# Linear attention, then a GELU layer: chunk 2's first product by seven half-size products throughout, with half of w_in's block sums formed during chunk 0

## The chip, the cores and the metric

The kernel runs on one core of one Trainium2 chip. A core has TensorE (PE in the profile; its weight loads are PEld), VectorE (DVE), ScalarE (ACT), GpSimd (POOL) and SyncE (SP), which here only issues DMAs. Matmuls write to PSUM, which has eight banks of 128 partitions x 512 fp32; POOL does not read them in this kernel. The metric is the device time of one execution in microseconds; less is better.

## The reference

```python
def _attn_ref(q, k, v):                      # 8 x 8 heads x 576 x 64
    q_s = np.exp(q - np.max(q, axis=-1, keepdims=True))
    q_s = q_s / (np.sum(q_s, axis=-1, keepdims=True) + 1e-09)
    k_s = np.exp(k - np.max(k, axis=2, keepdims=True))
    k_s = k_s / (np.sum(k_s, axis=2, keepdims=True) + 1e-09)
    kv = np.einsum('bhsd,bhse->bhde', k_s, v)
    return np.einsum('bhsd,bhde->bhse', q_s, kv)

x = attn_out.transpose(0, 2, 1, 3).reshape(4608, 512)
h = x @ w_in                                 # 512 x 2048
g = 0.5 * h * (1.0 + erf(h * inv_sqrt2))
return g @ w_out                             # 2048 x 512
```

Inputs and output are float32 in HBM. The kernel multiplies in bf16 and leaves out the subtraction of the maxima, which cancels.

## The kernel before

**Chunks.** The 4608 rows are worked on in nine chunks of 512. Chunk b (0 to 7) is the first 512 rows of batch b; chunk 8 is the 64 rows that each batch has left. A chunk goes through these steps: load q, k, v; exp of q and k on ScalarE (`exp_q`, `exp_k`), cast of v; `norm_q` (VectorE sums exp(q) over a head and takes the reciprocal, L260 and L261; POOL or VectorE multiplies, L262); transposition of q (on TensorE for chunks 0 and 1, by a DMA on SP from chunk 2 on, `xbar_step`, L312); k-v products (`kv_mm`, L225) with a column of ones in v that gives the sums of exp(k); `kv_norm` (reciprocal of that column, L239, and multiply, L240); x transposed (`x_mm`, L332), copied to SBUF by ScalarE (L359) and VectorE (L357) in four blocks of 128 model columns; h with GELU on ScalarE; then the output matmuls, and stores on SP. `manual_schedule` leaves every engine's instructions in the order in which the program writes them.

**h, plain.** Chunks 0 and 1, and half of chunk 2, form h by tiles of 128 of the 2048 columns: four matmuls of 512 columns (the rows of x) each over the four blocks of x (`h_mm`, L366), then one gelu (L372). Chunk 0 does so in `h_phase`, chunk 1 in `h_pairs` with three banks in turn.

**h, by half-size products.** `h_waves` forms h from chunk 2 on by the Winograd form of Strassen's scheme: instead of eight block products seven, each with 256 columns. The h tiles go in four blocks q = 0 to 3 (each: two tiles of the upper and two of the lower half of h). `mm(m, q)` is product m of block q: four matmuls (L486). It needs block sums of w_in (`quad_weights(w)`, four VectorE operations L419; w = 0 serves blocks 0 and 1, w = 1 blocks 2 and 3) and block differences of x (`x_sums`, four VectorE operations t1 to t4). Around the products: `seed` copies product 1 on ScalarE to a second bank (L494), before later products go on adding to the first; `p5_copy` brings product 5 to SBUF (L498); `e_sum` and `r_sum` are VectorE sums (L419) of two or three products; `gelu` finishes the four quarters C, r, B and A (L510). Products 1, 6, 7 and 4 of a block add up in one bank (A), 5, e and 3 use another (B), the seed and 2 a third (C). `roles` names the banks; some serve as C of one block and B of another: C of block 2 is B of block 0.

With `two` true (chunks 3 to 8) both halves of h go through this scheme. With `two` false (chunk 2), blocks 0 and 1 are eight plain tiles, and VectorE forms `quad_weights(0)` meanwhile; blocks 2 and 3 go by products.

**Output.** Chunk 0 multiplies plainly (L607): 16 h tiles x 4 row groups j, into four banks `yps` that the banks' rotation gives: 0, 1, 3, 4. Chunk 0's last h tiles 14 and 15 lie in banks 0 and 1. Among these output matmuls chunk 1's transposition, k-v products and x are placed (its transposes in banks 5 and 2), and chunk 1's first four h tiles lie in banks 0, 1, 3 and 4. From chunk 1 on `y_phase` forms the output by seven half-size products too (L664; `y_last`, L734, for chunk 8); its argument hangs further work behind numbered steps. In chunk 1 step 3 is the k-v step of chunk 2, exp(k) and `norm_q(3)`, whose multiply is POOL's; step 6, at the end, has load(4), x of chunk 2, the transposition of chunk 3's q, and the k-v step of chunk 3. In front of step 5 POOL forms two differences of the output (L419) that the stores wait for.

**Workspace.** The pool `wst` has five slots in rotation for raw weights and later for the sums: w_in parts 0 to 4, w_out parts 0 to 3, w16 (sums of w_out, `mix_wo`), quad_s of w = 1, quad r, quad t, quad_s of w = 0.

Of the kernel before, what the change touches and what calls it, by code (L numbers as in the profile page):

```python
# [8 lines left out]
FP32 = mybir.dt.float32  # L9
BF16 = mybir.dt.bfloat16  # L10
AF = mybir.ActivationFunctionType
ALU = mybir.AluOpType
# [4 lines left out]
def kernel(  # L17
# [212 lines left out]
    def kv_norm(b, half=None):  # L230

        if half is None:
            parts = [(ps, kvc[b][:, 2 * i:2 * i + 2], 2) for i, ps in enumerate(st[b]["kvall"])]
        else:
            parts = [(st[b]["kv"][hp].unsqueeze(1), kvc[b][:, hp:hp + 1], 1)
                     for hp in (2 * half, 2 * half + 1)]
        for src, dst, m in parts:
            rec = small.tile([128, 2], FP32, tag="reck")
            nc.vector.reciprocal(rec[:, 0:m], src[:, :, D])  # L239
            nc.vector.tensor_tensor(  # L240
                out=dst, in0=src[:, :, 0:D],
                in1=rec[:, 0:m].unsqueeze(2).to_broadcast([128, m, D]), op=ALU.mult,
            )
# [7 lines left out]

    def norm_q(b, i=0, n=1, eng=None):

        eng = eng or nc.gpsimd
        eq = st[b]["eq"]
        w = H // n
        hs = slice(i * w, (i + 1) * w)
        qsum = small.tile([128, J, w], FP32, tag="qsum")
        recq = small.tile([128, J, w], FP32, tag="recq")
        nc.vector.reduce_sum(out=qsum, in_=eq[:, :, hs, :], axis=AX.X)  # L260
        nc.vector.reciprocal(recq, qsum)  # L261
        eng.tensor_tensor(  # L262
            out=eq[:, :, hs, :], in0=eq[:, :, hs, :],
            in1=recq.unsqueeze(3).to_broadcast([128, J, w, D]), op=ALU.mult,
        )
# [95 lines left out]
    def h_begin(c):  # L361
        st[c]["g"] = moe_sb.tile([128, NDF, M], BF16, tag="g", name="g", bufs=1)
# [36 lines left out]
    def h_pairs(c, ins, done=()):  # L399


        if not done:
            h_begin(c)
        for p in range(HK):
            for t in (p + HK, p):
                if t in done:
                    continue
                ps = psum_h.tile([128, M], FP32, tag="h", name="ps")
                h_mm(c, ps, t, range(NDM))
                h_gelu(c, ps, t)  # L410
            if p in (1, 3, 5):
                s_ops(c, p - 1, 2)
            elif p > 5:
                s_ops(c, p, 1)
            for f in ins.get(p, []):
                f()
# [36 lines left out]
    def h_waves(c, two, sums):  # L453
# [38 lines left out]
        def seed(q):  # L492
            take("C", q)
            nc.scalar.copy(out=held["C", q], in_=held["A", q])  # L494

        def p5_copy(q, eng):
            held["r", q] = quad["r"][:, q]
            eng(out=held["r", q], in_=held["B", q])  # L498

        def e_sum(q):  # L500
            tt(held["B", q], held["A", q], held["r", q])
# [11 lines left out]
        if two:  # L513
            mm(1, 0, 1)
            seed(0)
            mm(5, 0, 1)
            seed(1)
            p5_copy(0, scopy)
            p5_copy(1, scopy)
            mm(6, 0, 1)  # L520
            x_sums(c, (3,))
            e_sum(0)
            e_sum(1)
            x_sums(c, (4,))
            mm(2, 0, 1)
            gelu("C", 0, 1)
            mm(7, 0, 1)
            r_sum(0)
            r_sum(1)
            mm(3, 0, 1)  # L530
            for q in (2, 3):
                mm(5, q)
                mm(1, q)
            mm(4, 0, 1)
            gelu("r", 0)
            gelu("B", 0, 1)
            gelu("r", 1)
            seed(2)
            seed(3)
            gelu("A", 0, 1)  # L540
            p5_copy(2, vcopy)
            p5_copy(3, vcopy)
            s_parts(c, 0, 4, (3,))
        else:
            turn = Banks(*(roles[n] for n in ("bb", "kv0", "kv1", "x0")))
            x_sums(c, (1, 2, 3, 4))
            for p in range(HK // 2):
                for t in (p + HK, p):
                    ps = turn.tile([128, M], FP32)
                    h_mm(c, ps, t, range(NDM))  # L550
                    h_gelu(c, ps, t)
                if p == 1:
                    s_parts(c, 0, 2, (0, 1))
                    for fn in sums:
                        fn()
            mm(1, 2, 3)
            seed(2)
            seed(3)
            mm(5, 2, 3)
            p5_copy(2, vcopy)  # L560
            p5_copy(3, scopy)
# [3 lines left out]
        if two:  # L565
            s_parts(c, 0, 4, (4,))
# [10 lines left out]
        if two:  # L577
            s_parts(c, 0, 4, (0,))
        else:
            s_parts(c, 2, 2, (0, 1))  # L580
# [346 lines left out]
    def ybank():  # L927
        return psum_y.tile([128, M], FP32, tag="y", name="ps")

    h_phase(0, {  # L930
# [3 lines left out]
        9: [lambda: cast_wo(0, wo[0])],  # L934
# [14 lines left out]
    w16 = wst.tile([128, 2, HK, HN], BF16, tag="w", name="w16")  # L949
    mix_wo(6, 0)  # L950
    mix_wo(6, 1)
# [3 lines left out]
    tps = [pool.tile([128, HP, J, 64], BF16, tag=tag, name="tp")  # L955
           for pool, tag in ((psum_a, "a"), (psum_h, "h"))]
    yps = [psum_h.tile([128, DM], FP32, tag="h", name="ps") for j in range(2)]
    yps += [psum_y.tile([128, DM], FP32, tag="y", name="ps") for j in range(2)]
# [25 lines left out]
    x_tile(1, 0, psum_a, "a")  # L984
    x_tile(1, 1, psum_h, "h")
# [11 lines left out]
    hps = [psum_h.tile([128, M], FP32, tag="h", name="ps") for t in range(2)]  # L997
    hps += [psum_y.tile([128, M], FP32, tag="y", name="ps") for t in range(2)]
# [8 lines left out]
    x_evac(1, 3)  # L1007
    for t in range(2, 4):
        h_mm(1, hps[t], t1s[t], (0, 1))
    for t in range(4):  # L1010
# [8 lines left out]
    sums = quad_weights(1)  # L1019
# [3 lines left out]
    h_pairs(1, h1, done=t1s)  # L1023
# [10 lines left out]
        3: [lambda: kv_step(2), lambda: exp_k(3), lambda: norm_q(3)],  # L1034
        4: [lambda: table(AF.Gelu)],
        6: [lambda: load(4), lambda: x_all(2, (3, 4, 1, 5)), lambda: xbar_step(3), lambda: kv_step(3)],
    })
    quad["r"] = wst.tile([128, 4, 2, HT], FP32, tag="w", name="r")
    quad["t"] = wst.tile([128, 4, 2, HT], BF16, tag="w", name="quad_t")
    sums = quad_weights(0)  # L1040


# [16 lines left out]
    for c in range(2, B + 1):  # L1059
        nb = c + 2  # L1060
        if 2 < c and nb < B:
            load(nb)
        elif nb == B:
            load_qrest()
        h_waves(c, c > 2, sums)
        s_parts(c, 4, 4, (2,))
        yi = {}
        if nb <= B:
            yi[8] = [lambda: exp_q(nb)]
            yi[1] = [lambda: norm_q(nb)]  # L1070
            yi[3] = [lambda: table(AF.Gelu)]
        if nb < B:
            yi[9] = [lambda: exp_k(nb)]
            yi[0] = [lambda: touch_g(c), lambda: cast_v_all(nb)]
        if c < B:
            yi[5] = [lambda: next_x(c, nb)]
            y_phase(c, yi)
        else:
            y_last(c)
# [30 lines left out]
```

## Time and profile before

| what | value |
|---|---|
| time, median of 3 runs (lowest, highest) | 259.36 us (259.2, 259.4) |
| the profiled execution's time | 259.4 us |
| its span, first to last instruction | 257.6 us |
| mean granted clock of TensorE | 0.995 |
| DMA queue q1 | 49.39 MB, 56.9% of 16 engines' span |
| HBM read, written | 36.70 MB, 9.44 MB |
| chunk 0's h matmuls (L366) | 64 in 13.99 us |
| gelu of a plain h tile (L372), mean | 600 ns |
| one half-size matmul (L486) on the row, mean | 273 ns |
| seed (L494), p5 copy on ScalarE (L498), mean | 577 ns, 610 ns |
| e sum, r sum on VectorE (L419), mean | 694 ns, 685 ns |
| block sum of w_in on VectorE (L419), mean | 684 ns |
| POOL multiply of q, 128x2048 (L262, with the half-size ones), mean | 3046 ns |

A row of the profile gives line, engine, operation, tiles and shapes. Matmuls overlap: one of 512 columns shows 379 ns in its row, and 64 of them in a row take 13.99 us; times of TensorE's work are therefore taken from the chain of work that ended last, whose columns are start, duration, and what. In the timeline the columns are start, duration, engine, line, operation, tiles, and count; in square brackets is how long the engine stood idle before, and what released it.

### The profile page before, as it was taken

The numbers are of one execution on the slowest core, as the hardware profiler recorded it, in microseconds if no ns is written. First come the engines' busy times: TensorE is split into PE (matmuls) and PEld (weight loads), VectorE is DVE, ScalarE is ACT, GpSimd is POOL, SyncE is SP. The second block draws the span as 40 slices with busy tenths as digits, with TensorE's granted clock in tenths as the row PEclk, the third lists the DMA queues.
The fourth block names the chain that finished last, engine by engine and source line by source line (L and its number), as shares of the span: only waits on it lengthen the run. The fifth ranks groups of instructions, "written<-read, shape, count | busy, mean of one in ns | idle before, by whom it ended". The sixth has DMA issues, their size and how long they took to land.

```text
span 257.6 us, 6452 instructions
## 1 busy us (share of the span) xinstructions
PE 249.9 (97%) x2646; PEld 193.3 (75%) x2646; DVE 207.2 (80%) x360; ACT 187.8 (73%) x317; POOL 67.6 (26%) x64
## 2 busy tenths in 40 slices
PE   7899999999999999999999999999999999999992
PEld 3444445448856888888888888888888888888881
DVE  1877596998989988898889888988898889398961
ACT  4875986699967996889688968896886687158620
POOL 1530033000790058005800580058001800040000
PEclk9999999999999999999999999999999999999998
DMA  7999999992408964990499039904920440031024
GB/s 234 401 399 427 398 409 398 397 413 118 84 3 272 377 128 90 305 383 3 91 308 368 17 82 307 387 3 86 274 55 0 87 160 3 0 120 46 3 63 101
DMA packets 43165, 50.22 MB, mean 195 GB/s; under 512 B 20224, under 2 KB 30464, under 8 KB 42880
## 3 DMA queue, kind: packets, MB, share of 16 engines
q1 hardware_dynamic: 42736, 49.39, 56.9%
q10 hardware_dynamic: 400, 0.43, 0.7%
q8 instruction: 20, 0.33, 0.5%
q14 instruction: 9, 0.07, 0.1%
HBM read 36.70 MB, written 9.44 MB: 179 GB/s over the span
## 4 chain that ended last, share of the span: by engine, by line
PE 93%; DMA 4%; POOL 1%; ACT 0%; DVE 0%; issue 0%; SPq 0%
PE qa L486 18%; PE ps L366 14%; PE ya L664 10%; PE yd L664 9%; PE qb L486 9%; PE ye L664 5%; PE ps L607 5%; PE yb L664 5%; PE qc L486 4%; PE yx L664 4%; PE ps L332 2%; DMA f<-in_v_dram 2%; PE kv L225 2%; DMA f<-in_q_dram 2%; PE ya L734 1%; PE yd L734 1%
## 5 line engine op out<-in xcount | busy, mean ns | idle before, releaser
L664 PEld LDWEIGHTS <-g 128*128 128x128 bf16 x448 | 43.3, 98 | 5.8 <-issue 0.4
L262 POOL TENSOR_TENSOR e<-e,recq 128x2048 bf16<-128x2048 bf16 (+1 forms) x9 | 27.4, 3046 | 75.1 <-DVE recq L261 50.3
L486 PEld LDWEIGHTS <-quad_s 128*128 128x128 bf16 x416 | 40.7, 98 | 4.9 <-issue 0.2
L664 PEld LDWEIGHTS <-s 128*128 128x128 bf16 x336 | 32.8, 98 | 3.8
L366 PE MATMUL ps<-xT,wi_bf 128*128 128x512 bf16 x160 | 35.5, 379 | 0.1
L486 PEld LDWEIGHTS <-wi_bf 128*128 128x128 bf16 x312 | 30.5, 98 | 3.7
L366 PEld LDWEIGHTS <-wi_bf 128*128 128x128 bf16 x160 | 15.4, 98 | 19.2 <-issue 0.8
L372 ACT ACTIVATE g<-ps 128x512 bf16<-128x512 f32 x40 | 22.5, 600 | 9.1 <-PE ps L366 8.7
L486 PE MATMUL qa<-quad_t,quad_s 128*128 128x256 bf16 x208 | 27.1, 273 | 0.0
L419 POOL TENSOR_TENSOR y_sb<-y_sb 128x512 f32<-128x512 f32 x14 | 19.5, 1394 | 21.8 <-DVE y_sb L419 21.3
L260 DVE TENSOR_REDUCE qsum<-e 128x16 f32<-128x1024 bf16 (+1 forms) x12 | 20.9, 1738 | 4.9 <-ACT e L173 4.8
L494 ACT COPY qc<-qa 128x512 f32<-128x512 f32 x26 | 13.9, 577 | 11.5 <-PE qa L486 11.5
L173 ACT ACTIVATE e<-f 128x512 bf16<-128x512 f32 (+1 forms) x42 | 20.5, 556 | 1.5 <-DMA f<-in_q_dram 1.1
L510 ACT ACTIVATE g<-r 128x512 bf16<-128x512 f32 x26 | 16.2, 630 | 6.6 <-DVE r L419 6.6
L419 DVE TENSOR_TENSOR qb<-qa,r 128x512 f32<-128x512 f32 x26 | 16.9, 694 | 4.6 <-ACT g L510 3.1
L510 ACT ACTIVATE g<-qc 128x512 bf16<-128x512 f32 x26 | 14.1, 594 | 7.2 <-PE qc L486 7.2
L190 POOL CAST v_aug<-f 128x576 bf16<-128x576 f32 x26 | 17.6, 708 | 4.7 <-DMA f<-in_v_dram 4.7
L178 ACT ACTIVATE ek<-f 128x2304 bf16<-128x2304 f32 (+1 forms) x10 | 17.2, 1734 | 0.5 <-DMA f<-in_k_dram 0.5
L419 DVE TENSOR_TENSOR r<-qa,r 128x512 f32<-128x512 f32 x26 | 16.7, 685 | 0.7 <-PE qa L486 0.4
L391 DVE TENSOR_TENSOR s<-g 128x1024 bf16<-128x1024 bf16 x26 | 17.2, 686 | 0.0
L1046 POOL CAST scr<-g 128x1 f32<-128x1 bf16 x4 | 0.7, 187 | 58.6 <-DVE g L394 58.6
L607 PE MATMUL ps<-wo_bf,g 128*128 128x512 bf16 x64 | 14.5, 379 | 0.5 <-ACT g L372 0.5
(96 smaller groups left out, 477.7 us busy)
## 6 DMA issues: line engine op xcount, KB each, us to landing
out_dram<-y_sb SPq DMA_DIRECT2D x16, 512.0 KB, 3.8
f<-in_k_dram SPq DMA_DIRECT2D x6, 1152.0 KB, 9.7
f<-in_v_dram SPq DMA_DIRECT2D x6, 1152.0 KB, 11.7
f<-in_q_dram SPq DMA_DIRECT2D x6, 1024.0 KB, 8.0
w<-in_moe_w_in_dram SPq DMA_DIRECT2D x6, 512.0 KB, 8.7
f<-in_v_dram SPq DMA_DIRECT2D x8, 288.0 KB, 6.2
f<-in_q_dram SPq DMA_DIRECT2D x4, 512.0 KB, 8.9
w<-in_moe_w_out_dram SPq DMA_DIRECT2D x2, 1024.0 KB, 11.8
```

Of the source, the lines that this page charges most:

```text
L173: nc.scalar.activation(out=dst[:, i], in_=src[:, u], func=AF.Exp)
L178: nc.scalar.activation(out=ek[b % 2][:, i:i + n], in_=st[b]["kf"][:, i:i + n].rearrange("p x (n d) -> p x n d", n=NS), func=AF.Exp,)
L190: eng.tensor_copy(out=o, in_=i)
L260: nc.vector.reduce_sum(out=qsum, in_=eq[:, :, hs, :], axis=AX.X)
L262: eng.tensor_tensor(out=eq[:, :, hs, :], in0=eq[:, :, hs, :], in1=recq.unsqueeze(3).to_broadcast([128, J, w, D]), op=ALU.mult,)
L366: nc.tensor.matmul(ps, wi_bf[:, dm, t * 128:(t + 1) * 128], st[c]["xT"][:, dm, :], start=(dm == 0), stop=(dm == NDM - 1),)
L372: nc.scalar.activation(out=st[c]["g"][:, t, :], in_=ps, func=AF.Gelu)
L419: eng.tensor_tensor(out=out, in0=in0, in1=in1, op=op)
L486: nc.tensor.matmul(held[kind, q][:, u], w, mov[m][:, k], start=(m in (1, 5) and u == 0 and k == 0), stop=(k == 1), skip_group_check=True,)
L510: nc.scalar.activation(out=g[:, t:t + 2, half], in_=held[kind, q], func=AF.Gelu)
L607: nc.tensor.matmul(ps, st[c]["g"][:, t, j * 128:(j + 1) * 128], wo_bf[:, t, :], start=(t == 0), stop=(t == NDF - 1),)
L664: nc.tensor.matmul(ps[:, j * HN:(j + 1) * HN], act[m][:, k, j * 128:(j + 1) * 128], wgt[m][:, k, :], start=(first and k == 0 and j == 0), ...
```

## The change

- `kv_norm` for half a chunk's heads takes both reciprocals first and then both multiplies.
- `norm_q` is split in `q_sums` (VectorE) and `q_scale` (the multiply). For chunk 3, `q_sums` stays in chunk 1's `y_phase`; `q_scale` and `xbar_step` go to `q_late`, which is called inside chunk 2's `h_waves`; a small POOL copy there waits for the first p5 copy.
- `h_waves` has no plain tiles any more. In chunk 2 (`mid` given) products 1 of all four blocks come first, then 2, 5, and 6 of blocks 0 and 1, then product 5 of blocks 2 and 3; t1 and t2 are formed around `kv_step(3)` at the end of chunk 1's `y_phase`, t3 and t4 ahead of the e sums. Its p5 copies are all ScalarE's.
- `quad_weights(0)` is formed in chunk 0: two operations behind h tile 9, ahead of the cast of w_out's part 0, and two behind the first `mix_wo`.
- Chunk 0's output lies in banks 3, 4, 2, 0; chunk 1's transposes in 5 and 1; its first four h tiles in 3, 4, 1, 7; its other h tiles take banks 2, 0, 5, 6 in turn.

```diff
     def kv_norm(b, half=None):
...
+        if half is not None:
+            hps = (2 * half, 2 * half + 1)
             rec = small.tile([128, 2], FP32, tag="reck")
+            for i, hp in enumerate(hps):
+                nc.vector.reciprocal(rec[:, i:i + 1], st[b]["kv"][hp][:, D:D + 1])
+            for i, hp in enumerate(hps):
+                nc.vector.tensor_tensor(
+                    out=kvc[b][:, hp, :], in0=st[b]["kv"][hp][:, 0:D],
+                    in1=rec[:, i:i + 1].to_broadcast([128, D]), op=ALU.mult,
+                )
+            return
...
-    def h_waves(c, two, sums):
+    def h_waves(c, mid):
...
-        if two:
-            mm(1, 0, 1)
-            seed(0)
+        mm(1, 0, 1)
+        seed(0)
+        if mid:
+            seed(1)
+            mm(1, 2, 3)
+            mm(2, 0, 1)
+            gelu("C", 0, 1)
+            mm(5, 0, 1)
+        else:
             mm(5, 0, 1)
             seed(1)
-            p5_copy(0, scopy)
-            p5_copy(1, scopy)
-            mm(6, 0, 1)
-            x_sums(c, (3,))
-            e_sum(0)
-            e_sum(1)
+        p5_copy(0, scopy)
+        p5_copy(1, scopy)
+        mm(6, 0, 1)
+        x_sums(c, (3, 4) if mid else (3,))
+        e_sum(0)
+        e_sum(1)
+        if not mid:
             x_sums(c, (4,))
+        if mid:
+            mid()
+            mm(5, 2, 3)
+            p5_copy(2, scopy)
+            p5_copy(3, scopy)
+        else:
             mm(2, 0, 1)
             gelu("C", 0, 1)
...
+        mm(7, 0, 1)
+        r_sum(0)
+        r_sum(1)
+        mm(3, 0, 1)
+        if not mid:
             for q in (2, 3):
                 mm(5, q)
                 mm(1, q)
...
+        mm(4, 0, 1)
+        gelu("r", 0)
+        gelu("B", 0, 1)
+        gelu("r", 1)
+        seed(2)
+        seed(3)
+        gelu("A", 0, 1)
+        if not mid:
             p5_copy(2, vcopy)
             p5_copy(3, vcopy)
-            s_parts(c, 0, 4, (3,))
-        else:
-            turn = Banks(*(roles[n] for n in ("bb", "kv0", "kv1", "x0")))
-            x_sums(c, (1, 2, 3, 4))
-            for p in range(HK // 2):
-                for t in (p + HK, p):
-                    ps = turn.tile([128, M], FP32)
-                    h_mm(c, ps, t, range(NDM))
-                    h_gelu(c, ps, t)
-                if p == 1:
-                    s_parts(c, 0, 2, (0, 1))
-                    for fn in sums:
-                        fn()
-            mm(1, 2, 3)
...
+        s_parts(c, 0, 4, (3,))
         mm(6, 2, 3)
...
+    sums0 = quad_weights(0)
     h_phase(0, {
...
-        9: [lambda: cast_wo(0, wo[0])],
+        9: sums0[0:2] + [lambda: cast_wo(0, wo[0])],
...
     mix_wo(6, 0)
+    for fn in sums0[2:]:
+        fn()
     mix_wo(6, 1)
...
-    tps = [pool.tile([128, HP, J, 64], BF16, tag=tag, name="tp")
-           for pool, tag in ((psum_a, "a"), (psum_h, "h"))]
-    yps = [psum_h.tile([128, DM], FP32, tag="h", name="ps") for j in range(2)]
-    yps += [psum_y.tile([128, DM], FP32, tag="y", name="ps") for j in range(2)]
+    tps = [psum.tile([128, HP, J, 64], BF16, tag=f"k{i}", name="tp") for i in (5, 1)]
+    yps = [bank(i) for i in (3, 4, 2, 0)]
...
-    hps = [psum_h.tile([128, M], FP32, tag="h", name="ps") for t in range(2)]
-    hps += [psum_y.tile([128, M], FP32, tag="y", name="ps") for t in range(2)]
+    hps = [bank(i) for i in (3, 4)]
...
+    hps += [bank(i) for i in (1, 7)]
...
-    h_pairs(1, h1, done=t1s)
+    h_pairs(1, h1, done=t1s, turn=Banks(2, 0, 5, 6))
...
-        3: [lambda: kv_step(2), lambda: exp_k(3), lambda: norm_q(3)],
+        3: [lambda: kv_step(2), lambda: exp_k(3), lambda: q_sums(3)],
         4: [lambda: table(AF.Gelu)],
-        6: [lambda: load(4), lambda: x_all(2, (3, 4, 1, 5)), lambda: xbar_step(3), lambda: kv_step(3)],
+        6: [lambda: load(4), lambda: x_all(2, (3, 4, 1, 5)),
+            lambda: kv_step(3, lambda: x_sums(2, (1,))), lambda: x_sums(2, (2,))],
     })
...
+    def q_late():
+        nc.gpsimd.tensor_copy(out=scr[:, 2:3], in_=quad["r"][:, 0, 0, 0:1])
+        q_scale(3, nc.gpsimd)
+        xbar_step(3)
...
-        h_waves(c, c > 2, sums)
+        h_waves(c, q_late if c == 2 else None)
```

## Prediction

> **What bounds the kernel.** I read the engine totals first, then the chain of work that ended last in order of time, then the timeline of the stretches that the change touches.
>
> ```profile
> PE 249.9 (97%) x2646; PEld 193.3 (75%) x2646; DVE 207.2 (80%) x360; ACT 187.8 (73%) x317; POOL 67.6 (26%) x64
> ```
> ```profile
> 12.89 1.36 PE ps L332 x8
> ...
> 14.26 13.99 PE ps L366 x64
> 28.25 0.02 issue
> 28.27 0.60 ACT g L372
> 28.88 0.04 issue
> 28.92 12.03 PE ps L607 x55
> ...
> 73.34 1.12 PE ps L366 x4
> 74.46 0.01 issue
> 74.48 6.22 PE ps L366 x28
> 80.69 0.87 PE qa L486 x8
> ```
>
> From 12.42 us to 252.67 us the chain is TensorE almost without a break. So a step counts only if it takes matmul time out, or closes or opens a pause of TensorE. The chain shows the few pauses: at L332 eight matmuls take 1.36 where later groups of eight take 0.56; at 28.25 it goes over to ScalarE for a gelu; at 73.34 four matmuls take 1.12 where 64 in 13.99 give 0.218 each, so 0.87. An eight of 256-column products is 0.873 ("a unit" below: 14 of them in 12.23).
>
> **Chunk 0's output in other banks.** Before, the second output matmul needs bank 1, which the gelu of the last h tile (28.27 to 28.87) still reads. TensorE is done with h at 28.25, runs one output matmul (0.22, to 28.47) and goes on at 28.92: a pause of 0.45. Then 55 matmuls take 12.03 against 55 x 0.2177 = 11.97, so 0.06 at most is refill. After, the order is banks 3, 4, 2, 0; the last of them to come free is bank 0, read by the gelu of tile 14, which starts at 27.41 and lasts 0.60: long over when the fourth matmul is due at 28.9. Gain 0.45 to 0.51; I take **-0.48**. What is late next is the data behind it: the last two casts of w_out end at 40.92 and the last v casts at 42.60, both led by DMA; their users (the last tile's matmuls near 42.8, k-v matmuls at 43.90) move to about 42.2 and 43.3. Margin 0.7.
>
> **kv_norm, reciprocals first.** Only its half form (chunks 0 and 1) changes, and only chunk 0 has TensorE waiting for it.
>
> ```profile
> 12.37 0.17 DVE L239 RECIPROCAL rec<-kv 128x1 f32<-128x1 f32 x1 [0.61 <-PE kv L225]
> 12.57 0.22 DVE L240 TENSOR_TENSOR kvc<-kv,rec 128x64 bf16<-128x64 f32 x1
> 12.71 0.16 DVE L239 RECIPROCAL rec<-kv 128x1 f32<-128x1 f32 x1
> 12.90 0.22 DVE L240 TENSOR_TENSOR kvc<-kv,rec 128x64 bf16<-128x64 f32 x1
> ```
>
> A multiply starts 0.20 after its own reciprocal, but an independent operation 0.14 after the one in front. With both reciprocals first the second multiply would start at 12.37 + 3 x 0.14 = 12.79 instead of 12.90: 0.11 sooner. ScalarE's first x copy (13.63) and the first h matmul (14.26) follow it by as much. The trace has no two neighbouring reciprocals: at 0.20 apart nothing is gained; at 0.08 (what 0.16 leaves after the 0.08 that the row shows neighbours to overlap) the last multiply ends 0.26 sooner. Range 0 to 0.26; I take the row: **-0.11**. The Trainium skill (VectorE: DVE Perf Modes, The DRAIN you can't avoid) says that chained operations pay the flush whether or not a semaphore stands between them, so that only their count matters; by it this step would be worth 0. The starts 0.14 and 0.20 apart in these rows speak against it for such short operations, and taking it would raise the sum by 0.11.
>
> **w_in's sums for columns of chunk 2's first half.** Four operations of 0.685 (quad_s<-wi_bf) leave chunk 2 on VectorE for chunk 0. Two stand ahead of the cast of w_out's first quarter, which idled 1.43 for its DMA until 25.87: they need 1.37. Two stand after the first mix, where VectorE then idled 2.87 (for ScalarE's cast, until 30.69). Both covered: **0**. Without cover, the first pair would push that cast from 27.10 towards 28.5, 0.4 beyond the first output matmul. The workspace slots rotate otherwise, but each new owner's predecessor has been cast by then.
>
> **q's scaling and transposition of chunk 3, moved.** One POOL multiply (3.62 at 71.15) moves behind the first p5 copy of chunk 2 (about 77.2) and ends near 81; the transposing DMA on SP stands behind it, at about 81.2, now after load(4) as it was before (it was issued at 81.54 and done by 92). Its reader, chunk 3's x matmul, is at 97.29. On POOL the two output differences no longer wait behind the multiply, so chunk 1's stores and load(4), both queued on SP behind them, go some 3 us sooner. Nothing of this is on TensorE's path: **0**; it would cost only if the transposition came 5 us later than now. Chunk 1's four h banks instead of three: its last 60 h matmuls run 13.06, 0.218 each, so there was no wait to remove: **0**.
>
> **Chunk 2.** Before, eight plain tiles take from 73.34 to 80.69 = 7.35 (32 matmuls are 6.99; the rest is the wait for kv_norm's bank at 74.47 and the refill). After, seven products of two blocks take 7 units = 6.11. Gain **-1.24**. The first product needs only x blocks 0 and 1 (VectorE's first copy ends at 73.40): no wait worth counting. VectorE's differences, e and r sums are each ready 0.2 or more ahead of their product. But look at product 6 of blocks 2 and 3. It accumulates onto banks that ScalarE must first copy (the seed, L494), and the seeds stand behind four gelus. Chunk 3 of before has that same ScalarE order:
>
> ```profile
> 103.72 1.04 PE L486 MATMUL qa<-quad_t,quad_s 128*128 128x256 bf16 x8
> 104.36 1.29 DVE L419 TENSOR_TENSOR r<-qa,r 128x512 f32<-128x512 f32 x2
> 105.08 0.63 ACT L510 ACTIVATE g<-r 128x512 bf16<-128x512 f32 x1 [0.43 <-DVE r L419]
> 105.61 1.07 ACT L510 ACTIVATE g<-qb 128x512 bf16<-128x512 f32 x2
> 106.57 0.63 ACT L510 ACTIVATE g<-r 128x512 bf16<-128x512 f32 x1
> 107.09 1.08 ACT L494 COPY qc<-qa 128x512 f32<-128x512 f32 x2
> ```
>
> Product 7's first half ends at 103.88 (the chain's start of that piece) + 0.44 = 104.32; the first seed ends at 107.09 + 0.60 = 107.69: 3.37 of r sum, gelu r, two gelus B, gelu r, seed, without a hole on ScalarE. In chunk 3 TensorE has between them the other half of product 7 (0.44), product 3 (0.87), products 5 and 1 of blocks 2 and 3 (1.75) and product 4 (0.87): 3.93, so it never waits. In the new chunk 2, products 1 and 5 of blocks 2 and 3 have been drawn ahead and 0.44 + 0.87 + 0.87 = 2.18 is left. TensorE stands for 3.37 - 2.18 = 1.19, plus 0.05 from gelu end to matmul (28.87 to 28.92) and 0.06 of refill: **+1.30**. Behind the seeds on ScalarE stand only gelus A, which nobody awaits sooner than in chunk 3. Lower end 1.1 (no latency, sum a little sooner), upper 1.7 (the POOL multiply now runs beside the e and r sums; a sum like theirs, y_sb<-zeros,ya, runs up to 0.07 longer beside POOL than its mean 0.62, and four of them and some jitter make 0.4).
>
> **Sum**: -0.48 - 0.11 - 1.24 + 1.30 = -0.53. The profiled execution took 259.4, of it 257.6 the span and 1.8 around it; the median of the runs is 259.36. So span 257.1 and a time of **258.8**. A measurement can tell about 0.2% = 0.52 from no change, so the forecast lies on that line.
>
> **Rivals.**
> Full gain in chunk 2: the seeds end before product 6 is due, because products 1 and 5 drawn ahead also let ScalarE run ahead. For it: ScalarE waits in chunk 3 (2.16 ahead of its first seeds). Against: the 3.37 starts from product 7, which TensorE itself makes. Time 258.83 - 1.30 = 257.5; chance 0.15.
> The front's gain is caught by DMA: until 60 us the engines move some 400 GB/s, and if v or w_out rows land 0.7 later than now, TensorE gives its 0.59 back in chunk 0. Against: the margins above. Time 259.4; chance 0.10.
> Slower: POOL's multiply, now beside chunk 2's e and r sums, slows VectorE as it does elsewhere: quad_t<-xT took 0.41 with POOL idle (77.61) and 0.89 beside POOL (101.47). If the two e sums and first r sum went from 0.65 to 1.4, product 7 and with it the 3.37 come some 2 later: 258.83 + 2.0 = 260.8. It decides from about 1 us of delay. Against: sums that read PSUM hardly stretch (0.69 beside POOL). Chance 0.10.
> Slower: the pause makes the granted clock fall. The core's mean clock is 0.995, so all that the throttle took from this execution is 0.005 x 257.6 = 1.3; one more loss of that size gives 258.83 + 1.3 = 260.1. Against: the window from 24 to 30 us, with TensorE busy 5.53 of 6, still shows a clock of 1.00. Chance 0.05. The Trainium skill (TensorE: Matmul & The Clock Gate, HAM oscillation) lets the clock fall at idle gaps beyond some 3.4 us; by it a pause like this one costs no clock, and the trace agrees as far as its 0.47 goes.
>
> **How the numbers follow.** The forecast has 0.60, its own range 258.4 to 259.2, split by 258.84 almost evenly. Faster: 0.31 + 0.15 = 0.46; within 0.2%: 0.29 + 0.10 = 0.39; slower: 0.15. The range takes in the first three cases, 257.4 to 259.9, and leaves out 0.15.
>
> **What would show it.** In the changed profile: no gelu in the chain near 28 us and output matmuls in one row; the first L366 near 14.15; in chunk 2 TensorE idle of about 1.2 released by ScalarE's copy L494, ahead of product 6 of blocks 2 and 3; the first yd of chunk 2 about 0.5 sooner than 86.81, and every later chunk by the same. Wrong would be: no such idle (then chunk 2 gains 1.2), idle released by VectorE's sums, or a pause between 40 and 44 us behind a DMA.

## The result, and the profile after

The changed kernel takes **260.72 us** (median of its runs, 260.65 to 260.85) against 259.39 for the kernel before in the same comparison: 1.0052 times as long, 95% interval 1.0039 to 1.0065. It is slower by 0.5%, where 258.8 was forecast with a range of 257.4 to 259.9. Two single executions of the runs below, of 433 us (e4) and 655 us (e2), are left out of the ratios. The profiled execution took 260.76 with a span of 259.0, which is 1.4 more than the 257.6 of before; the granted clock is 0.994 against 0.995.

The engine totals and the instruction queue, from the page of the changed kernel:

```profile
PE 248.7 (96%) x2664; PEld 195.8 (76%) x2670; DVE 207.9 (80%) x362; ACT 189.7 (73%) x322; POOL 68.7 (27%) x65
...
q8 instruction: 21, 0.34, 0.5%
```

TensorE is busy for 1.2 us less, as planned, and the span is longer all the same. The chain of waits of the changed kernel, in order of time (start, length, engine, tile, line), shows where the time went:

```profile
14.17 0.81 PE ps L377 x3
...
28.18 0.60 ACT g L383
28.78 1.79 ACT wo_bf L843
30.60 0.69 DVE w L861
31.29 1.21 DVE quad_s L428 x2
32.49 0.60 DVE w L861
...
37.12 1.90 POOL e L269
39.03 2.42 POOL v_aug L190 x2
41.49 0.47 PE kv L225 x31
...
59.02 1.75 PE yd L666 x16
...
73.36 1.93 PE qa L495 x16
...
80.04 2.12 ACT g L519 x4
82.16 0.50 ACT qc L503
82.70 1.08 PE qa L495 x8
...
87.27 1.75 PE yd L666 x16
...
253.27 0.42 DVE y_sb L428
```

Before, TensorE stood in this chain without a break from 28.92. Now the chain leaves it twice: from 28.18 to 41.49 it runs through ScalarE, VectorE and POOL, and from about 79.3 to 82.70 through VectorE and ScalarE. Third, the end: VectorE's last sum ends at 253.27 + 0.42 = 253.69, and the span goes on to 259.0. With the same points of both profiles (the first h matmul; the first matmul into the tile yd, with which a chunk's output products begin, of chunks 1, 2 and 3; the end of the last sum), in us:

| stretch | before | after | difference | predicted |
|---|---|---|---|---|
| to the first h matmul | 14.26 | 14.17 | -0.09 | -0.11 |
| chunk 0, to the first yd of chunk 1 | 44.74 | 44.85 | +0.11 | -0.48 |
| to the first yd of chunk 2 | 27.81 | 28.25 | +0.44 | +0.06 |
| to the first yd of chunk 3 | 25.80 | 25.91 | +0.11 | 0 |
| to the end of the last sum | 140.5 | 140.5 | 0 | 0 |
| the tail: from there to the end of the span | 4.49 | 5.31 | +0.82 | 0 |

Chunk 0 gave back the whole gain of its banks, chunk 2 lost 0.4 more than worked out, and most of the loss stands at the end of the kernel, where the change edits nothing.

**Chunk 0.** VectorE in the kernel before, and then ScalarE, VectorE and TensorE in the changed one, from their timelines (start, busy time, engine, line; in brackets the idle time ahead and what ended it):

```profile
27.13 0.69 DVE L859 TENSOR_TENSOR w<-wo_bf 128x1024 bf16<-128x1024 bf16 x1
30.69 0.69 DVE L859 TENSOR_TENSOR w<-wo_bf 128x1024 bf16<-128x1024 bf16 x1 [2.87 <-ACT wo_bf L841]
```
```profile
28.68 1.89 ACT L843 CAST wo_bf<-w 128x2048 bf16<-128x2048 f32 x1
...
30.60 0.69 DVE L861 TENSOR_TENSOR w<-wo_bf 128x1024 bf16<-128x1024 bf16 x1 [3.21 <-ACT wo_bf L843]
31.21 0.69 DVE L428 TENSOR_TENSOR quad_s<-wi_bf 128x1024 bf16<-128x1024 bf16 x1
...
41.49 0.47 PE L225 MATMUL kv<-v_aug,ek 64*64 64x65 bf16 x34 [0.58 <-POOL v_aug L190]
```

The first mix of w_out, which ran at 27.13 before, now waits until 30.60 for ScalarE's cast of another quarter, which it doesn't use. Its output tile w16 has been given the workspace slot of that quarter, and the cast is the slot's last reader. The built programs show the slots: w16 has the address of w_out's part 1, 176896; before it had that of w_in's part 4, 152320, which now goes to the sums. So the slots aren't handed out in plain rotation, as the section on the workspace has it; in rotation w16 would have had the slot of w_out's part 0 (144128), whose cast on VectorE ends at 27.39, just ahead of the mix. The two sums meant for the idle time stand behind the waiting mix, so they come after the idle time and not in it. POOL's multiply follows at 37.12 (before 35.41), and TensorE waits for POOL's cast of v, 0.58 at 41.49.

**Chunk 2.** The pause is the one forecast:

```profile
82.05 1.08 ACT L503 COPY qc<-qa 128x512 f32<-128x512 f32 x2
82.70 1.08 PE L495 MATMUL qa<-quad_t,quad_s 128*128 128x256 bf16 x8 [1.29 <-ACT qc L503]
```

It is 1.29, released by the seed, ahead of product 6 of blocks 2 and 3. Two smaller losses stand beside it in the chain. The first 16 products take 1.93 instead of 1.75: the second of them starts 0.20 behind the first instead of 0.11, at 73.49, when VectorE's first x copy has ended (73.44); the other half is what a row of 16 behind k-v products costs elsewhere too (at 99.00 they take 1.85). And the eight from 82.70 take 1.08 instead of 0.87. Of these 0.21, 0.05 is a wait for the second seed, which ends at 83.13 (the product behind it starts at 83.18, 0.16 after the one ahead instead of 0.11). The other 0.16 is refill: the first product behind a pause takes 0.27 to its end, and in a row they follow each other by 0.11.

**The tail.** SP issues the output's last stores. From the timelines of SP, first the kernel before, then the changed one:

```profile
248.73 0.47 SPq L725 DMA_DIRECT2D out_dram<-y_sb  x1
249.24 0.59 SPq L725 DMA_DIRECT2D out_dram<-y_sb  x1
249.93 0.55 SPq L725 DMA_DIRECT2D out_dram<-y_sb  x1
```
```profile
249.29 0.47 SPq L727 DMA_DIRECT2D out_dram<-y_sb  x1
249.81 1.62 SPq L727 DMA_DIRECT2D out_dram<-y_sb  x1
251.53 0.55 SPq L727 DMA_DIRECT2D out_dram<-y_sb  x1
```

In these rows a store's issue takes 0.47 to 0.59; the one at 249.81 takes 1.62, and those behind it are late. In the DMA view of the changed kernel from 249.5 to 250.0, one packet stands that the kernel before doesn't have there:

```profile
q8 instruction: 1, 0.02, 17.2%
```

It is a 16 KB block of instructions, the 21st, in transfer from 249.68 to 251.06; the kernel before fetches 20, the last at 238.93.

### The profile page after: what moved, and what is told of

The parts are those of the page before. It is cut to its first block, busy times and chain, and to the rows that moved or that the text cites. A ratio compares the mean times of both kernels' runs of the same rounds, so it can differ in the third digit from the quotient of the medians.

```text
span 259.0 us, 6509 instructions
## 1 busy us (share of the span) xinstructions
PE 248.7 (96%) x2664; PEld 195.8 (76%) x2670; DVE 207.9 (80%) x362; ACT 189.7 (73%) x322; POOL 68.7 (27%) x65
## 4 chain that ended last, share of the span: by engine, by line
PE 86%; DMA 4%; DVE 3%; POOL 2%; ACT 2%; issue 0%; SPq 0%; DVEq 0%; POOLq 0%
PE qa L495 19%; PE ps L377 11%; PE ya L666 10%; PE yd L666 9%; PE qb L495 9%; PE ye L666 5%; PE qc L495 5%; PE yb L666 5%; PE yx L666 4%; PE kv L225 2%; DMA f<-in_v_dram 2%; PE ps L343 2%; DMA f<-in_q_dram 2%; POOL v_aug L190 1%; PE ya L736 1%; PE yd L736 1%
## 5 line engine op out<-in xcount | busy, mean ns | idle before, releaser
L495 PEld LDWEIGHTS <-quad_s 128*128 128x128 bf16 x448 | 43.8, 98 | 6.8 <-issue 1.6
L495 PE MATMUL qa<-quad_t,quad_s 128*128 128x256 bf16 x224 | 29.3, 272 | 1.3 <-ACT qc L503 1.3
L377 PE MATMUL ps<-xT,wi_bf 128*128 128x512 bf16 x124 | 27.7, 379 | 0.3
L428 DVE TENSOR_TENSOR qb<-qa,r 128x512 f32<-128x512 f32 x28 | 18.3, 694 | 6.1 <-ACT g L519 3.1
L519 ACT ACTIVATE g<-r 128x512 bf16<-128x512 f32 x28 | 17.4, 630 | 7.5 <-DVE r L428 7.5
L383 ACT ACTIVATE g<-ps 128x512 bf16<-128x512 f32 x32 | 17.7, 601 | 6.2 <-PE ps L377 5.9
L402 DVE TENSOR_TENSOR s<-g 128x1024 bf16<-128x1024 bf16 x28 | 18.6, 683 | 1.6 <-ACT g L519 1.6
L428 DVE TENSOR_TENSOR r<-qa,r 128x512 f32<-128x512 f32 x28 | 18.0, 684 | 0.7 <-PE qa L495 0.4
L495 PE MATMUL qb<-quad_t,quad_s 128*128 128x256 bf16 x112 | 15.5, 273 | 0.0
L495 PE MATMUL qa<-xT,wi_bf 128*128 128x256 bf16 x112 | 15.4, 273 | 0.0
```

Source lines behind the costliest of these rows:

```text
L377: nc.tensor.matmul(ps, wi_bf[:, dm, t * 128:(t + 1) * 128], st[c]["xT"][:, dm, :], start=(dm == 0), stop=(dm == NDM - 1),)
L383: nc.scalar.activation(out=st[c]["g"][:, t, :], in_=ps, func=AF.Gelu)
L402: tt(out=s12[:, a, half], in0=g[:, a, half], in1=g[:, b, hi], op=ALU.add)
L428: eng.tensor_tensor(out=out, in0=in0, in1=in1, op=op)
L495: nc.tensor.matmul(held[kind, q][:, u], w, mov[m][:, k], start=(m in (1, 5) and u == 0 and k == 0), stop=(k == 1), skip_group_check=True,)
L519: nc.scalar.activation(out=g[:, t:t + 2, half], in_=held[kind, q], func=AF.Gelu)
```

## The experiments

Three suspicions follow: the slot in chunk 0, the order around the seeds in chunk 2, and the instruction block at the end. Each was tried alone, on the changed kernel or on the one before, and then together. All ratios are to the kernel before.

**e1_slot: two allocations exchanged, to give w16 another slot.**

```diff
-    w16 = wst.tile([128, 2, HK, HN], BF16, tag="w", name="w16")
     sums = quad_weights(1)
+    w16 = wst.tile([128, 2, HK, HN], BF16, tag="w", name="w16")
     mix_wo(6, 0)
```

> The changed kernel with one pair of lines exchanged: the workspace for w_in's sums of w = 1 is taken ahead of w16, so that w16 gets the slot of w_out's part 0 (cast by VectorE) instead of part 1 (cast by ScalarE). Theory: in the changed kernel the first w_out mix and the two sums behind it wait for ScalarE's cast (idle 3.2 us until 30.60), VectorE's chain and POOL's multiply come 1.7 us later, and TensorE pays 0.58 at the k-v products near 41.5. Then here the mix starts near 27.4, that wait is gone, the first yd of chunk 1 starts near 58.4 instead of 59.02, and the time falls by 0.5 to 0.6 to about 260.15. Rival (the front is led by DMA rows of v, as the prediction's second rival has it): the wait near 41.5 stays, the time stays at 260.7.

Measured 260.55, ratio 1.0043 (1.0030 to 1.0056), and 44.84 from the first h matmul to yd of chunk 1: nothing changed there. A miss of the edit and not of the theory: in the built program w16 lies at the same address as in the changed kernel, and the mix still waits for ScalarE's cast (3.83, until 31.13). It tells only that the order in which slots are asked for doesn't alone decide who gets which.

**e2_after_pad and e3_before_pad: small matmuls in the warm-up.** They shift every later TensorE instruction by a number of places, e2 on the changed kernel and e3 on the one before.

```diff
-    warm(7, zeros32)
+    pads = bank(7, "pad")
+    for i in range(64):
+        nc.tensor.matmul(pads[:, 0:64], identity, identity[:, 0:64], start=True, stop=True)
+    warm(1, zeros32)
```

(e3: 28 of them and `warm(4, zeros32)`.)

> The changed kernel with 64 small matmuls into an unused bank ahead of the warm-up, and one warm-up matmul instead of seven: some 100 more TensorE instructions, in time that TensorE spends waiting for q. Theory: the changed kernel loses some 0.8 us after its last matmul, because the transfer of a 16 KB block of instructions (queue 8) now falls at 249.7, where SP issues the last stores, and one store's issue takes 1.62 instead of 0.59. With the instructions shifted, that transfer comes about 5.5 us sooner, no store issue near the end is above 0.75, and the time falls by 0.7 to 0.9 to about 259.9. Rival (the longer tail comes from the stores themselves, the order of the engines or the chip): the tail keeps its 5.3 us from the last VectorE sum to the span's end, the time stays at 260.7.

> The kernel before with 28 small matmuls into an unused bank ahead of the warm-up, and four warm-up matmuls instead of seven; nothing else. TensorE's instructions are then as many as in the changed kernel. Theory of the instruction block: a block's transfer now falls near 249 us, among the last stores, one store's issue takes over 1.2, and the time rises by 0.5 to 0.9, to about 260.1, with every matmul of the chunks where it was. Rival (the tail has nothing to do with instructions): within 0.2 of the kernel before.

e2: 261.2, ratio 1.0062 (1.0049 to 1.0075). Its only trace is that of the execution of 655 us, which can't tell what the stores did, and the other four executions had a mean clock of 0.983 to 0.985, so the time is no answer either. Inconclusive. e3: 260.99, ratio 1.0066 (1.0047 to 1.0086), on a kernel whose computation is the one of before. SP's timeline of e3:

```profile
249.58 0.47 SPq L725 DMA_DIRECT2D out_dram<-y_sb  x1
250.10 1.67 SPq L725 DMA_DIRECT2D out_dram<-y_sb  x1
```

The long issue is there, with an instruction block in transfer from 250.28 to 251.37, and the tail is 5.33 instead of 4.49. But the thinner warm-up also cost something of its own: the mean clock fell to 0.991 (0.50 from 13 to 15 us), and chunk 0 took 45.18 instead of 44.74. So e3 has the long tail with a block beside its stores and nothing else of the change, but its time is a sum of two things. The later runs keep the warm-up long.

**e4_seeds: in chunk 2 the gelus of B and the seeds ahead of the gelus of r, the first seed by VectorE.**

```diff
-        gelu("r", 0)
-        gelu("B", 0, 1)
-        gelu("r", 1)
-        seed(2)
-        seed(3)
+        if mid:
+            gelu("B", 0, 1)
+            seed(2, vcopy)
+            seed(3)
+            gelu("r", 0, 1)
+        else:
...
         gelu("A", 0, 1)
```

> The changed kernel, with chunk 2's seeds of blocks 2 and 3 drawn ahead: gelus B of blocks 0 and 1 first, then the seed of block 2 by VectorE and that of block 3 by ScalarE, then gelus r. Theory: the pause of TensorE ahead of product 6 of blocks 2 and 3 (1.29, released by ScalarE's seed) goes down to 0.1 or 0.2, nothing else waits in its place, the first yd of chunk 2 comes 1.1 to 1.4 sooner, the time falls by as much, to about 259.4. Rival: the pause moves, to product 6's second block or to the r sums behind VectorE's seed, and half or less of it is won: 260.1 or more.

Measured 260.46, ratio 1.0042 (1.0027 to 1.0056); yd of chunk 1 to yd of chunk 2 takes 28.24, as in the changed kernel. The pause of 1.29 is gone, and another has come. From its timeline:

```profile
82.57 0.69 DVE L402 TENSOR_TENSOR s<-g 128x1024 bf16<-128x1024 bf16 x1 [1.45 <-ACT g L519]
...
83.92 1.20 PE L495 MATMUL qa<-quad_t,quad_s 128*128 128x256 bf16 x8 [0.85 <-DVE qb L428]
```

On VectorE the s sum now waits 1.45 for the gelus of r that were moved back, and the e sums of product 7 stand behind it. The wait went to the next place. Chunk 0, which the edit leaves alone, took 58.67 - 13.83 = 44.84.

**e6_seeds_s3: e4, and the s sum behind the r sums.** Added to the diff of e4:

```diff
-        s_parts(c, 0, 4, (3,))
+        if not mid:
+            s_parts(c, 0, 4, (3,))
         mm(6, 2, 3)
...
         r_sum(3)
+        if mid:
+            s_parts(c, 0, 4, (3,))
         gelu("r", 2, 3)
```

> The changed kernel with gelus B and the seeds of blocks 2 and 3 drawn ahead as in the run of the seeds, and with VectorE's s sum (part 3), which there stood in front of the e sums and held product 7 for 0.85, put behind the r sums of blocks 2 and 3. Theory: from chunk 1's first yd to chunk 2's it takes 27.0 to 27.2 instead of 28.25, the time falls by about 1.1. Rival (ScalarE's gelus r and A, now later, hold product 4 or the first output product instead): 27.7 or more, the time falls by half of it or less.

Measured 259.34, ratio 1.0002 (0.9993 to 1.0011). Its chain of waits:

```profile
80.50 0.61 ACT g L519
81.13 0.71 DVE qc L503
81.88 1.03 PE qa L495 x8
...
86.41 1.75 PE yd L675 x16
```

The product that waited 1.29 now follows the one ahead of it (80.74 + 1.04) after 0.1. The stretch is 27.02: 1.23 less than in the changed kernel and 0.79 less than before.

**e5_sums_first: the two sums ahead of the first mix.**

```diff
-    mix_wo(6, 0)
     for fn in sums0[2:]:
         fn()
+    mix_wo(6, 0)
     mix_wo(6, 1)
```

> The changed kernel, with chunk 0's second pair of w_in sums ahead of the first w_out mix instead of behind it (exchanging the two allocations, the run before, left w16 in the slot of w_out's part 1, so this is tried by order instead). Theory: the pair then runs from about 27.4 in the time in which VectorE waits for ScalarE's cast, VectorE's chain behind 30.6 comes 1.2 us sooner, the wait of TensorE at the k-v products near 41.5 (0.58) is gone, the time from the first h matmul to chunk 1's first yd falls from 44.85 to about 44.3, and the time by 0.5 to 0.6. Rival (v's rows or another cast hold the front): the wait stays, the time is that of the changed kernel.

Measured 259.80, ratio 1.0020 (1.0011 to 1.0028). The timeline of VectorE and the chain of waits of e5:

```profile
27.42 0.68 DVE L428 TENSOR_TENSOR quad_s<-wi_bf 128x1024 bf16<-128x1024 bf16 x1
28.02 0.69 DVE L428 TENSOR_TENSOR quad_s<-wi_bf,quad_s 128x1024 bf16<-128x1024 bf16 x1
30.59 1.29 DVE L861 TENSOR_TENSOR w<-wo_bf 128x1024 bf16<-128x1024 bf16 x2 [1.89 <-ACT wo_bf L843]
```
```profile
14.14 13.92 PE ps L377 x64
28.07 12.09 PE ps L609 x56
40.15 0.64 PE tp L307 x64
...
58.20 1.75 PE yd L666 x16
```

The slot is still the same and the mix still waits, but the sums use the wait. TensorE goes from h into the output matmuls without a gap and reaches yd 44.06 after the first h matmul: 0.79 less than in the changed kernel.

**e7_front_alone: the kernel before, with only kv_norm and the banks changed.** kv_norm, the `bank(...)` and `Banks(...)` lines and the `turn` argument of the change, on the kernel before; no sums in chunk 0, chunk 2 as it was.

> The kernel before with two parts of the change alone: kv_norm's reciprocals first, and the banks of chunk 0's output and chunk 1's h tiles; w_in's sums stay in chunk 2, which is as before. Theory: the prediction's front terms hold where nothing is put into VectorE's chain of chunk 0: 0.45 to 0.51 for the banks and 0.1 to 0.2 for kv_norm, no wait at the k-v products near 41, the time falls by 0.55 to 0.7 to about 258.8; TensorE's instructions are as many as before, so the tail stays 4.5. Rival (DMA leads the front, whatever VectorE does): a wait near 41 to 44, the time falls by less than 0.2.

Measured 258.52, ratio 0.9968 (0.9957 to 0.9980): faster than the kernel before, by 0.3%. Chunk 0 takes 44.11 (before 44.74), the other stretches are those of before (27.81, 25.80), and the tail is 4.54 with no instruction block in it.

**e8_before_block and r3_after_block: extra TensorE instructions, with a warm-up that stays long.** e8 puts 38 bf16 matmuls of 384 columns in place of the 7 float32 ones of the kernel before; r3 puts 64 of 256 columns into the changed kernel (its lines are shown). Both leave the computation alone.

```diff
-    warm(7, zeros32)
+    zb = singles.tile([128, 512], BF16, name="zb")
+    nc.vector.memset(zb, 0.0)
+    pads = psum_y.tile([128, DM], FP32, tag="y")
+    for i in range(64):
+        nc.tensor.matmul(pads[:, 0:256], zb[:, 0:128], zb[:, 0:256], start=True, stop=True)
```

> The kernel before with its warm-up of seven fp32 matmuls replaced by 38 bf16 matmuls of 384 columns on zeros (the run with 28 small ones had a longer store issue and tail, but also a colder start): some 50 to 70 more TensorE instructions, the start as it was. Theory of the instruction block: a block is transferred at 248 to 250, a store issued then takes over 1, the stretch from the last VectorE sum to the span's end grows from 4.5 by 0.4 to 0.9, and the time by as much, unless the block falls between 248.0 and 249.2, where SP issues nothing. Rival: tail and time as before, within 0.2.

> The changed kernel with the same warm-up and nothing else. Theory of the instruction block: chunks as in the changed kernel, tail 4.5 instead of 5.31, time about 260.0 instead of 260.7. Rival: tail above 5.0, time 260.5 or more.

e8: 260.12, ratio 1.0038 (1.0025 to 1.0051). r3: 260.07, ratio 1.0027 (1.0017 to 1.0037), 0.65 less than the changed kernel's 260.72, though its first h matmul comes 0.41 later. SP's timelines of e8 and of r3:

```profile
248.56 0.47 SPq L725 DMA_DIRECT2D out_dram<-y_sb  x1
249.07 1.30 SPq L725 DMA_DIRECT2D out_dram<-y_sb  x1
250.47 0.55 SPq L725 DMA_DIRECT2D out_dram<-y_sb  x1
```
```profile
249.60 0.47 SPq L727 DMA_DIRECT2D out_dram<-y_sb  x1
250.11 0.59 SPq L727 DMA_DIRECT2D out_dram<-y_sb  x1
250.80 0.55 SPq L727 DMA_DIRECT2D out_dram<-y_sb  x1
```

The two runs cross over. The kernel before, with every stretch as it was (44.74, 27.81, 25.80), gets the long issue with a block at 248.97 and a tail of 5.15. The changed kernel, with the block moved to 245.28, loses it, and its tail is 4.51. With more TensorE instructions one kernel gets a longer tail and the other a shorter one, so it isn't their number that costs here, but the place of the block.

**r1_both, r2_both_block, r4_both_short: the mends together.** r1 is e5 and e6 in one; r2 adds the warm-up of 64 matmuls of 256 columns, and r4 that of 64 with 176.

> The changed kernel with both mended parts at once: chunk 0's second pair of sums ahead of the first w_out mix, and in chunk 2 gelus B and the seeds drawn ahead with the s sum behind the r sums. Theory (the parts add): 44.1 from the first h matmul to chunk 1's first yd, 27.0 on to chunk 2's, a tail of 5.1 to 5.3; against the kernel before -0.2 (kv_norm) -0.65 -0.8 +0.1 (chunk 3) +0.7 (tail) = about -0.85, so 258.5. Rival (the front's gain collides with something in chunk 2, or the reverse): 259.0 or more.

> The same, with the warm-up as 64 bf16 matmuls of 256 columns on zeros: by the rows 100 more TensorE instructions than the changed kernel has, so that the last block of instructions comes some 5.5 us sooner, near 243 instead of 249. Theory of the instruction block: no store issue after 248 takes over 0.8, the tail falls to 4.5, the time to about 257.8, the fastest of all. Rival (the tail belongs to the longer TensorE program or to the stores' order, not to where the block falls): the tail stays above 5.0, the time is that of the run without it.

> The kernel with both sequences mended (two of w_in's sums ahead of the first mix, the s sum behind the r sums) and the same number of extra warm-up matmuls, 64, of 176 columns instead of 256. If the instruction block alone sets the long tail, the number of TensorE instructions is the same as with 256 columns, so the tail stays near 4.4 us (5.1 without the extra instructions) and no store issue on SP takes over 0.8. The longer warm-up ended at 11.77 and put the first h matmul to 14.81; 64 x 0.075 = 4.8 us from 4.8 would end near 9.6, ahead of the first transposes at 10.0, so the first h matmul is back near 14.2 and the span is 256.7 - 0.6 = 256.1, the time 257.8 (ratio 0.994). Rival: the tail depends on the time at which the block is fetched and not on the count alone; then a start 0.6 earlier moves the block against the stores and the tail is anywhere between 4.4 and 5.1, time up to 258.5. Second rival: the smaller matmuls warm TensorE less, the granted clock falls to 0.991 as where the warm-up was thinned, and yd of chunk 1 minus the first h matmul is 44.4 instead of 44.06.

| kernel | time | ratio (interval) | span | first h | chunk 0 | to yd of chunk 2 | tail |
|---|---|---|---|---|---|---|---|
| r1 | 258.62 | 0.9972 (0.9964 to 0.9981) | 256.8 | 14.21 | 44.06 | 27.02 | 5.09 |
| r2 | 258.39 | 0.9962 (0.9950 to 0.9974) | 256.7 | 14.81 | 44.11 | 27.02 | 4.44 |
| r4 | 257.82 | 0.9957 (0.9939 to 0.9974) | 255.9 | 13.98 | 44.10 | 27.02 | 4.49 |

The mends add up. From the changed kernel's span, 259.0 - 0.79 (sums) - 1.23 (seeds) - 0.22 (tail) = 256.8 is what r1 has. r1 still has a block at 247.76 and beside it a store issue of 1.22. In r2 the tail is mended, but the warm-up runs until 11.77, over the start of the first transposes, and the first h matmul is 0.6 later. In r4 the warm-up ends at 9.24, ahead of them; its DMA view from 242 to 243 has the block, well ahead of the last stores:

```profile
q8 instruction: 1, 0.02, 6.1%
```

r4 has the shortest time of all, faster than both kernels; its interval is too wide to put it ahead of r2 for certain. The table's stretches are of an execution with a clock of 1.000. Five of r4's twelve executions had a mean clock of 0.985 to 0.989 and took 258.45 to 260.39, the other seven 0.994 to 1.000 and 257.60 to 257.93; so the second rival of its expectation, the smaller warm-up, came true in part of them.

## Why the prediction was wrong

**The step that failed** is the one on w_in's sums: "Two stand after the first mix, where VectorE then idled 2.87 ... Both covered: 0", with its reason, "The workspace slots rotate otherwise, but each new owner's predecessor has been cast by then". For w16 it doesn't hold: its predecessor is w_out's part 1, which ScalarE casts until 30.57, and the first mix was due at 30.60 - 3.21 = 27.39. In plain rotation the sentence would have held for it. It turned the 2.87 of cover into a wait at the head of the queue with the sums behind it. e5, which moves only these two sums, gives 0.79 back in chunk 0, and e7, without sums, reaches the same 44.1. The prediction had named a pause between 40 and 44 us behind a DMA as a sign of being wrong. The pause came, at 41.49, but its cause was VectorE's lateness, handed on through POOL's v cast.

**What the sum did not contain** is the tail, the largest single term (+0.82). Here the premise failed that "a step counts only if it takes matmul time out, or closes or opens a pause of TensorE": the late stores touch neither, and the span still ends later. e8 and r3 show that it belongs to the place of an instruction block among the last stores. The change comes into it only by its 24 matmuls and 24 weight loads more in the program (PE and its loads from 2646 and 2646 records to 2664 and 2670; some records are missing). At eight matmuls and eight loads in 0.87 us, 48 instructions are an estimated 2.6 us. The trace has the 20th block at 237.21 instead of 238.93, in a kernel that by then runs half a microsecond later, and a 21st 12.5 behind it; the kernel before fetches no more. That the block is TensorE's is inferred, from the fact that it moves when only TensorE gets instructions; the trace doesn't name its owner.

**Mis-sized: chunk 2** (+0.44 instead of +0.06). The mechanism and its main term are right: TensorE stands, released by the seed, and e6 takes out 1.23 by moving what stood ahead of the seeds. That 1.29 was measured where 1.30 was written is in part luck: the 1.30 had 1.24 of standing and 0.06 of refill, and it was 1.29 of standing, 0.16 of refill and 0.05 at the second seed, 1.50 in all, inside the range of 1.1 to 1.7. Missing was the 0.18 at the first products ("no wait worth counting": half of it is a wait for VectorE's x copy).

**Mis-sized: the banks.** The gelu's pause near 28 us went as worked out, and the gain is larger: in e7 the 56 output matmuls of 28.51 to 40.59 take 12.08, where 28.25 to 40.95 was 12.70 before, so 0.62 against 0.48. The refill is the reason here too. Before, the first output matmul starts at 28.07 and the second at 28.92, 0.85 apart instead of 0.22, a loss of 0.63 where the prediction had 0.45 and at most 0.06.

**Mis-sized: kv_norm** (0.11). The trace of the changed kernel has the row that was missing, two neighbouring reciprocals:

```profile
12.48 0.23 DVE L236 RECIPROCAL rec<-kv 128x1 f32<-128x1 f32 x2 [0.61 <-PE kv L225]
12.68 0.35 DVE L238 TENSOR_TENSOR kvc<-kv,rec 128x64 bf16<-128x64 f32 x2
```

One takes 0.17, the other 0.15, both together 0.23, so they start 0.09 apart, and the upper end of the range was the right one. From the start of the last k-v products to the first h matmul it is 1.63 instead of 1.84, a gain of 0.21 (0.26 in e7). In the changed kernel 0.12 of it went to k-v products that began later, behind v's DMA. The prediction read the Trainium skill (VectorE: DVE Perf Modes, The DRAIN you can't avoid) as putting the step at 0; but the same section says that a next operation that isn't held starts earlier, and these two reciprocals, 0.09 apart, agree with that.

**Right**: the moved multiply and transposition of q cost nothing (the stretch from yd of chunk 2 moved by 0.11 with them and by the same 0.11 in e5 and r1; it is 25.80 in e4 and 25.81 in r2 with them in place), the clock didn't fall for the pause, and POOL beside chunk 2's sums didn't slow them (while its multiply runs, from 77.59 to 81.21, two e sums take 0.70 and 0.69 and two r sums 0.69 and 0.68; over all chunks their means are 694 and 684 ns). Of that 0.11, 0.07 lies at the eight products of 110.45, whose second half starts at 110.79, behind VectorE's second e sum (to 110.74). Why that sum is late stays open; the 0.11 goes away in r2, r3, r4 and e4.

**The rivals**: "Full gain in chunk 2" (-1.24) comes nearest in e6, with -0.79, so most of the gain was there for another order of the same work. The slower rivals named the wrong places: the 260.8 of the one with POOL lies next to the measured time, but its stretched sums are not in the trace. No rival had the slot or the block.

## What to carry to other kernels

Before work is moved into an engine's idle time, name what that idle time waits for and whether the instruction at its head will still be the same one: a tile that takes over a slot inherits the wait for the slot's last reader, on whatever engine. Moving a wait's cause ahead can put the wait on the next queue, so follow it until an engine that is free ends it (e4 and e6). And where a change of half a per cent is judged, look at the tail and at the instruction queue too: the place of one block of instructions made the tail 0.66 longer in one kernel (e8) and 0.80 shorter in the other (r3).

## What the hardware showed that was not expected

**Instruction fetches and stores.** In eight traces (the changed kernel, e1, e3 to e6, e8, r1) the transfer of an instruction block falls beside the sixth of the last sixteen stores. The issue of that store takes 1.13 to 1.67 instead of 0.59, it ends 0.37 to 0.40 behind the block's transfer in every one of them, and the tail is 5.09 to 5.33. In the five others (before, e7, r2, r3, r4) the last block is through by 246.55, no issue of the last stores takes over 0.74, and the tail is 4.44 to 4.54. Loads early in the kernel show the same: before, the issue at 16.43 takes 0.95 instead of the 0.33 of most runs and ends 0.37 behind a block of 16.13 to 17.01. Overlap alone isn't enough: in r3 the store at 246.10 takes 0.56 beside a block of 245.28 to 246.55. The Trainium skill (Runtime: NRT & Kernel Launch, Instruction fetch mechanics) has the size of the block right, 16 KB, and calls the crossing mostly hidden. For TensorE it is hidden here (beside the changed kernel's block its matmuls start 0.11 apart without a gap); for the stores at the end it isn't. Why the issue of a store waits for it, no run shows.

**Warm-up.** Where the warm-up was thinned (e3, its last matmul ends at 7.80), the clock was 0.87 from 10 to 13 us, 0.50 from 13 to 15 and 0.84 from 15 to 17, and chunk 0 took 45.18 instead of 44.74. With 64 bf16 matmuls of 176 columns, 7.2 us in all (r4), the trace has a mean clock of 1.000, and chunk 0 took the same 44.1 as in r2, whose warm-up lasted 9.7. But five of r4's executions stayed at 0.985 to 0.989, where all of r1's and r2's have 0.993 or more; no trace of the five shows where their clock fell.
